# Expert 0's early rows grow from 256 to 384, and the row splits move ahead of the weight conversion, in an attention, mixture-of-experts and MLP kernel

## The chip, the cores and the metric

The kernel runs on one core of a Trainium2 chip. Its five engines each work through their own stream in order: TensorE (PE) multiplies, VectorE (DVE), ScalarE (ACT) and GpSimd (POOL) work on tiles, SyncE (SP) issues DMAs. The metric is the time of one execution on the device in microseconds, the median of several.

## The reference

The inputs are all float32. Sliding-window attention (window 128, ALiBi slopes) over 4 batches, 8 heads and 576 positions of 64 gives 2304 tokens of 512. Each token goes to two of eight experts, and a dense MLP follows:

```python
attn_out = _attn_ref(**attn_kwargs)
x = attn_out.transpose(0, 2, 1, 3).reshape(B * S, H * D)      # 2304 x 512
noisy = x @ w_gate + log1p(exp(x @ w_noise)) * noise          # 2304 x 8
top2, top2_w = the two largest of noisy and their softmax
for e in range(8):                                            # F = 1024
    for k in range(2):
        mask = top2[:, k] == e
        out[mask] += top2_w[mask, k, None] * (relu(x[mask] @ w1[e]) @ w2[e])
h = relu(out @ w_in)                                          # 2048 wide
return h * h @ w_out
```

## The kernel before

**Arithmetic.** A float32 operand is held as two parts, a rounded one (written by ACT) and the remainder (a subtraction on DVE or POOL). A product is three matmuls (`mm3`, L734). So each weight tile needs an ACT cast (L725) and a subtraction on DVE or POOL (L729; POOL does it in four pieces), and each tile of 126 or 128 token rows a cast and a DVE subtraction (`split_x`, L758 and L759, tile `turned`). This last pair is called the row split below.

**Stages.** Attention runs for 18 row tiles. Beside it, a side stream of small steps routes each group of tiles: `logits` and `route` find a token's two experts and its slot in each expert's list, POOL scatters the token numbers to `ids_dram`. The code is written with generators; each `yield` hands the turn back, and `wait` yields five times so that an engine further on has finished. Then come the experts. For each expert 630 slots are computed, in five row tiles.

**Expert 0** starts before all tokens are routed. Its first 256 rows come from the tokens of the first 12 row tiles (`EARLY`, `ET`): `early_rows` loads their list positions, gathers the rows by an indirect DMA on POOL's queue and joins the two 16-bit planes in which rows are stored (`together`, L427); `early_turn` transposes them on PE into the tile `x` or `ps_x` and splits them. `first_expert` then runs all eight slices f of the hidden dimension on these 256 columns (the early stage: `hA` 128x256 and `y` for two row tiles), then the same on the other 374 columns (the late stage: `hA` 128x374 and `y` for three row tiles). The late rows are gathered once all tokens are routed, joined, transposed and split in `late_turn`. Behind the late stage is a branch (`overflow`, L866), which ACT and the others reach in their own order.

**Experts 1 to 7** run one iteration for each slice f. PE does `hA` (374 columns), `hB` (256 columns), then the second product of the slice before (`y`, five row tiles, 15 matmuls). The tile `hB` has one PSUM buffer. Beside this, `fetch` gathers the next expert's rows, transposes them by DMA, and `prepare` joins one row tile (ACT, L427) and splits the one joined an iteration earlier. At f=7 the fifth and last row tile is split. The results `y` are copied out of PSUM after f=7, tiles 0, 2, 4 by ACT and 1, 3 by DVE (L838).

**The conversion.** The dense MLP's weights arrive as 64-bit floats; 32 half tiles are converted to float32 in 32 of the iterations (`HALVES`: six of every eight), by one ACT pass (L1092) and six DVE instructions (`convert_half`, L1104 to L1109). The order on PE, DVE, ACT and SP is the order in which the program is written; POOL's is set by a scheduler.

Of the kernel before, what the change touches and what calls it, by code (L numbers as in the profile page):

```python
# [8 lines left out]
F32 = mybir.dt.float32  # L9
# [12 lines left out]
P = 128  # L22
# [16 lines left out]
EARLY, ET = 12, 2  # L39
# [13 lines left out]
def wait():  # L53

    for _ in range(HOP):
        yield
# [16 lines left out]
class Kernel:  # L73
# [363 lines left out]
    def logits(self, x, lgs):  # L437
# [9 lines left out]
        lg = self.ps_tr.tile([P, 2 * NE], F32, name="ps_lg", tag="ps_tr")  # L447
# [5 lines left out]
    def route(self, vt0, n, lgs):  # L453
# [41 lines left out]
        while self.counted < vt0:  # L495
            yield
# [63 lines left out]
    def attention(self):  # L560
# [58 lines left out]
        def finish(vt, x):  # L619
# [123 lines left out]
    def gather(self, e, j, known=NT):  # L743
        xg = self.rwork.tile([P, DM], F32, name="x", bufs=XB)
        self.nc.gpsimd.indirect_dma_start(
            out=xg.bitcast(U16), out_offset=None, in_=self.x_dram[:known * P, :],
            in_offset=bass.IndirectOffsetOnAxis(ap=self.ids[:, e, j, 0:1], axis=0))
# [77 lines left out]
    def expert_b(self, e, fs, js=range(5)):  # L825

        nc = self.nc
        for j in js:
# [7 lines left out]
            if fs[-1] == 7:  # L836
# [4 lines left out]
                    out_offset=bass.IndirectOffsetOnAxis(ap=self.ids[:n, e, j, 1:2], axis=0),  # L841
# [9 lines left out]
    def count_tiles(self, counts):  # L851
# [5 lines left out]
        nc.vector.tensor_scalar(tiles[:, NE:NE + 1], counts[:, 1, 0:1], float(EARLY_ROWS), float(ET),  # L857
                                op0=ALU.is_lt, op1=ALU.mult)
# [53 lines left out]
    def load_ids(self, e, j0, j1):  # L912

        rows = self.ids_dram[e * REG + j0 * P:e * REG + j1 * P, :]
        self.nc.sync.dma_start(self.ids[:, e, j0:j1], rows.rearrange("(j p) o -> p j o", p=P))

    def early_rows(self):

        while self.scattered < EARLY:
            yield  # L920
        for _ in range(10):
            yield
        self.load_ids(0, 0, ET)
        for _ in range(14):
            yield
        for j in range(ET):
            self.xg[j] = self.gather(0, j, EARLY)
            yield
        for _ in range(8):
            yield  # L930
        for j in range(ET):
            x = self.rwork.tile([P, DM], F32, name="x", bufs=XB)
            self.xg[j] = self.together(self.xg[j], x, self.nc.vector.tensor_copy)
            yield
# [7 lines left out]
    def early_step(self, i):  # L942
# [3 lines left out]
        elif i == 4:  # L946
            self.early_turn(0)
            self.early_turn(1)
            self.split_weights(2, self.nc.vector)

    def settle(self):
# [4 lines left out]
        tot = self.ps_tr.tile([P, 2, NE], F32, name="ps_tot", tag="ps_tr")  # L956
        for i, vt in enumerate((NT, EARLY)):
            nc.tensor.matmul(tot[:, i, :], self.ones16, self.before[:, vt, :], start=True, stop=True)
        yield from wait()
        counts = self.const.tile([P, 2, NE], I32, name="counts")  # L960
# [272 lines left out]
```

## Time and profile before

| | before |
|---|---|
| three runs | 1108.34, 1106.16, 1117.47 us (median 1108.34) |
| the profiled execution | 1101.99 us, its span 1100.2 us |
| PE busy | 1036.5 us, 94% of the span |
| DVE, ACT, POOL busy | 534.4, 485.2, 483.5 us (49, 44, 44%) |
| mean granted clock of PE | 0.957 of full speed |
| attention until | about 206 us |
| expert 0, early stage, then late stage | 208.5 to 234.6 us, 246.5 to 279.9 us |
| experts 1 to 7 | from 283.3 us |

A row of a timeline gives the start, the duration, the engine with the line and the operation, what it writes and reads, and in brackets how long the engine had been idle before and which instruction ended that. A row of the waits adds such idle times up by pair. PE carries nearly all of the span, so a microsecond counts only where PE waits, or where PE runs below its full clock.

### The profile page before, as it was taken

What the parts mean: (1) busy time and instruction counts of PE and PEld (TensorE: products, weight loads), DVE (VectorE), ACT (ScalarE), POOL (GpSimd) and SP (SyncE); (2) the same over time, 40 slices, a digit from 0 to 9 for tenths busy, and PEclk for the clock granted to TensorE, in tenths of its full rate; (3) what the DMA queues carried; (4) which work ended last, traced back from release to release, by engine and by line L of the source; (5) the groups of instructions that cost most, each with busy time, mean ns of one, the idle gap of its engine ahead of it and who ended that gap; (6) DMA issues with size and microseconds to landing.
All of it is one profiled execution on the core that took longest, in us unless ns stands there. A gap on an engine that the chain in (4) does not pass through costs nothing.

```text
span 1100.2 us, 17058 instructions
## 1 busy us (share of the span) xinstructions
PE 1036.5 (94%) x6264; PEld 931.6 (85%) x6264; DVE 534.4 (49%) x1353; ACT 485.2 (44%) x897; POOL 483.5 (44%) x558
## 2 busy tenths in 40 slices
PE   4798989979899999998999999999999999999998
PEld 3687778869788989897888988899999999999997
DVE  7779687642357576756574421562232322223211
ACT  4678586435345454543453532553333333323322
POOL 5356464434466676665566563322222222222221
PEclk7879898789999999998999999999999999999999
DMA  9999993266495958586767422211212221031101
GB/s 200 173 177 207 192 170 102 79 151 158 129 208 172 212 185 215 192 216 188 185 170 199 113 67 72 72 39 34 73 20 67 48 68 39 10 83 33 29 1 29
DMA packets 204269, 131.43 MB, mean 119 GB/s; under 512 B 123108, under 2 KB 180580, under 8 KB 204176
## 3 DMA queue, kind: packets, MB, share of 16 engines
q1 hardware_dynamic: 195312, 109.39, 42.3%
q0 software_dynamic: 8864, 20.86, 6.9%
q8 instruction: 51, 0.84, 0.3%
q14 instruction: 42, 0.34, 0.1%
HBM read 84.56 MB, written 19.95 MB: 95 GB/s over the span
## 4 chain that ended last, share of the span: by engine, by line
PE 58%; DVE 5%; DMA 4%; issue 3%; POOL 2%; ACT 1%; SPq 0%; POOLq 0%; ACTq 0%; DVEq 0%
PE y L734 30%; PE h L734 18%; PE hA L734 6%; PE hB L734 5%; DMA raw<-in_moe_w_out_dram 2%; DVE turned L759 1%; POOL ring L729 1%; DMA y_dram<-xT,ids 1%; DVE raw L1108 1%; DVE store L1105 1%; DVE store L1106 1%; DMA raw<-in_moe_w_in_dram 1%; DVE raw L1107 1%; POOL first L729 0%; DVE hh L820 0%
## 5 line engine op out<-in xcount | busy, mean ns | idle before, releaser
L1141 POOL TENSOR_TENSOR hh<-relu,hh 128x384 fp32r<-128x384 f32 x96 | 97.2, 1013 | 296.9 <-ACT hh L1140 296.9
L1138 DVE SCALAR_TENSOR_TENSOR relu<-h,relu 128x384 f32<-128x384 f32 x96 | 53.5, 557 | 246.6 <-ACT relu L1137 246.6
L734 PE MATMUL y<-first,hh 128*126 128x512 f32 (+2 forms) x642 | 158.8, 396 | 0.0
L734 PE MATMUL y<-ring,hh 128*126 128x512 f32 (+1 forms) x612 | 151.7, 396 | 0.3 <-POOL hh L1141 0.3
L734 PEld LDWEIGHTS y<-first,hh 128*126 128x126 f32 (+2 forms) x642 | 117.7, 188 | 24.4 <-ACT hh L819 0.3
L734 PEld LDWEIGHTS y<-ring,hh 128*126 128x126 f32 (+1 forms) x612 | 112.9, 189 | 23.7 <-POOL hh L1141 0.8
L1137 ACT ACTIVATE relu<-h 128x384 f32<-128x384 f32 x96 | 47.1, 491 | 192.8 <-PE h L734 192.8
L729 POOL TENSOR_TENSOR first<-raw,first 128x256 fp32r<-128x256 f32 x116 | 97.0, 866 | 68.7 <-ACT first L725 55.6
L729 POOL TENSOR_TENSOR ring<-raw,ring 128x256 fp32r<-128x256 f32 x108 | 93.3, 893 | 52.1 <-ACT ring L725 41.7
L734 PE MATMUL y<-store,hh 128*128 128x512 f32 (+1 forms) x444 | 114.7, 397 | 0.0
L734 PE MATMUL h<-turned,store 128*128 128x384 f32 x552 | 107.4, 337 | 0.0
L734 PEld LDWEIGHTS h<-turned,store 128*128 128x128 f32 x552 | 98.1, 188 | 4.0
L734 PEld LDWEIGHTS y<-store,hh 128*128 128x128 f32 (+1 forms) x444 | 83.7, 190 | 15.3
L820 DVE SCALAR_TENSOR_TENSOR hh<-hA,hh 128x374 fp32r<-128x374 f32 (+3 forms) x76 | 39.8, 523 | 99.6 <-ACT hh L819 99.4
L734 PE MATMUL hA<-turned,first 128*128 128x374 f32 (+3 forms) x444 | 82.0, 335 | 4.2 <-ACTq L866 3.5
L734 PEld LDWEIGHTS hA<-turned,first 128*128 128x128 f32 x444 | 76.7, 194 | 7.9 <-ACTq L866 3.9
L1140 ACT CAST hh<-relu 128x384 fp32r<-128x384 f32 x96 | 49.3, 514 | 69.3 <-DVE relu L1138 65.5
L734 PE MATMUL hA<-turned,ring 128*128 128x374 f32 (+3 forms) x420 | 74.6, 327 | 0.0
L734 PEld LDWEIGHTS hA<-turned,ring 128*128 128x128 f32 x420 | 70.5, 188 | 3.0
L353 ACT ACTIVATE prob<-neg,least 128x256 f32<-128x256 f32 (+2 forms) x144 | 61.4, 473 | 9.3 <-DVE least L346 7.7
L759 DVE TENSOR_TENSOR turned<-x,turned 128x504 fp32r<-128x504 f32 (+2 forms) x41 | 41.1, 1004 | 47.3 <-ACT turned L758 47.1
L359 PE MATMUL ps_pt<-identf,prob 128*128 128x128 f32 (+1 forms) x256 | 49.2, 315 | 14.4 <-DVE den L408 11.4
(202 smaller groups left out, 1952.1 us busy)
## 6 DMA issues: line engine op xcount, KB each, us to landing
raw<-in_moe_w_dram SPq DMA_DIRECT2D x128, 256.0 KB, 3.7
raw<-y_dram SPq DMA_DIRECT2D x18, 512.0 KB, 4.0
raw<-in_moe_w_in_dram SPq DMA_DIRECT2D x16, 512.0 KB, 5.7
raw<-in_moe_w_out_dram SPq DMA_DIRECT2D x16, 512.0 KB, 5.8
vraw<-in_v_dram SPq DMA_DIRECT2D x36, 128.0 KB, 5.5
x_dram<-xn SPq DMA_DIRECT2D x18, 256.0 KB, 3.3
out_dram<-osb SPq DMA_DIRECT2D x36, 128.0 KB, 2.4
qraw<-in_q_dram SPq DMA_DIRECT2D x7, 512.0 KB, 4.9
```

The source lines that it names most:

```text
L353: self.nc.scalar.activation(u.p[:, a, :u.w], u.neg[:, a, :u.w], AF.Exp, bias=u.least[:, a:a + 1], scale=-1.0)
L359: self.nc.tensor.transpose(u.pt[:n, a, ci, :], u.p[:, a, ci * P:ci * P + n], self.identf)
L729: engine.tensor_sub(w[1][:, c], raw[:, c], w[0][:, c])
L734: self.nc.tensor.matmul(out, a(x), b(y), start=first and i == 0, stop=last and i == 2)
L759: self.nc.vector.tensor_sub(dst[:, 1, :, col:col + n], x[:, :, :n], dst[:, 0, :, col:col + n])
L820: nc.vector.scalar_tensor_tensor(hh[:, 1], ps, 0.0, hh[:, 0], op0=ALU.max, op1=ALU.subtract)
L1105: nc.vector.tensor_scalar(a, a, 3, 0x3FFFFFFF, op0=ALU.logical_shift_left, op1=ALU.bitwise_and)
L1106: nc.vector.scalar_tensor_tensor(a, hi, -0x40000000, a, op0=ALU.bitwise_and, op1=ALU.bitwise_or)
L1137: nc.scalar.activation(r, ps, AF.Relu)
L1138: nc.vector.scalar_tensor_tensor(r, ps, 0.0, r, op0=ALU.max, op1=ALU.mult)
L1140: nc.scalar.copy(hh[:, 0, :], r)
L1141: nc.gpsimd.tensor_sub(hh[:, 1, :], r, hh[:, 0, :])
```

## The change

Six things change together.

- `EARLY` becomes one number of known row tiles for each early tile (12, 12 and 14), and the early rows 384. Tile 2 is gathered once 14 row tiles are routed, and joined at the start of expert 0, right ahead of its transposes. The late stage keeps 246 columns, two row tiles.
- `route` is stepped by `paced`: three of its small steps a turn instead of one, while `wait` still waits whole turns.
- The logits go into the PSUM tile of the transposes.
- Expert 0's list positions get a tile of their own, `ids0`.
- The fetching of expert 1's rows starts one turn earlier, and its `prepare` follows after two turns instead of three.
- In `experts`, `prepare` (the row split) is written ahead of `convert_half`.

```diff
-EARLY, ET = 12, 2
+EARLY = 12, 12, 14
+ET = len(EARLY)
...
     for _ in range(HOP):
-        yield
+        yield True
+def paced(steps, n=3):
+    i = 0
+    for turn in steps:
+        i = (i + 1) % n
+        if turn or i == 0:
+            yield
...
-        lg = self.ps_tr.tile([P, 2 * NE], F32, name="ps_lg", tag="ps_tr")
+        lg = ps[:, 0, :2 * NE]
...
-                routes.append(self.route(starts[g], GROUPS[g], mine))
+                routes.append(paced(self.route(starts[g], GROUPS[g], mine)))
...
-        self.ids = self.const.tile([P, NE, 5, 2], I32, name="ids")
+        self.ids0 = self.const.tile([P, 5, 2], I32, name="ids0")
+        self.ids = self.const.tile([P, NE - 1, 5, 2], I32, name="ids")
...
     def early_rows(self):
-        while self.scattered < EARLY:
-            yield
-        for _ in range(10):
-            yield
-        self.load_ids(0, 0, ET)
...
+        for known in sorted(set(EARLY)):
+            js = [j for j in range(ET) if EARLY[j] == known]
+            while self.scattered < known:
+                yield
+            for _ in range(10):
+                yield
+            self.load_ids(0, js[0], js[-1] + 1)
+            for _ in range(14):
+                yield
+            for j in js:
+                self.xg[j] = self.gather(0, j, known, self.y_tile())
+                yield
+            if known < EARLY[-1]:
+                for _ in range(16):
+                    yield
+                for j in js:
+                    self.early_join(j)
+                    yield
+    def early_join(self, j):
+        x = self.rwork.tile([P, DM], F32, name="x", bufs=XB)
+        self.xg[j] = self.together(self.xg[j], x, self.nc.vector.tensor_copy)
...
-        elif i == 4:
-            self.early_turn(0)
-            self.early_turn(1)
+        for j in range(ET):
+            if i == (4 if EARLY[j] == EARLY[-1] else 3):
+                if i == 4:
+                    self.early_join(j)
+                self.early_turn(j)
+        if i == 4:
             self.split_weights(2, self.nc.vector)
...
                 for j in rest:
                     self.late_turn(j)
+                self.fetch(1, 0)
...
         self.expert_b(0, (7,), early)
-        self.fetch(1, 0)
         self.expert_a(0, 0, (1,))
         for f in range(8):
+            self.fetch(1, f + 1)
...
-            self.fetch(1, f + 1)
-            self.prepare(1, f + 1, 3)
+            self.prepare(1, f + 1)
...
+            if e + 1 < NE:
+                self.prepare(e + 1, f)
             if n - 1 in HALVES:
                 self.convert_half(HALVES.index(n - 1))
-            if e + 1 < NE:
-                self.prepare(e + 1, f)
```

The first place is DVE where attention ends and expert 0 starts. `turned<-ps_x` is the subtraction of an early row split, `den`, `x` and `xn` finish the last attention tile, `sp_` and `oh` are routing. Before:

```order
696 L422 COPY xn<-x 128x1024
697 L498 TENSOR_TENSOR before<-before,m 128x8
698 L464 TENSOR_SCALAR sp_u<-sp_e 128x8
699 L498 TENSOR_TENSOR before<-before,m 128x8
700 L502 TENSOR_TENSOR gd<-top 128x2
701 L759 TENSOR_TENSOR turned<-ps_x,turned 128x4x128 x2
702 L729 TENSOR_TENSOR first<-raw,first 128x1024
```

And in the changed kernel (the line numbers are those of its own text; L770 is L759 before, L438 is L427, L740 is L729):

```order
697 L770 TENSOR_TENSOR turned<-ps_x,turned 128x4x128 x2
698 L419 TENSOR_TENSOR den<-ps_av,eps 128x4
699 L421 RECIPROCAL den<-den 128x4
700 L423 TENSOR_TENSOR x<-ps_av,den 128x256
701 L433 COPY xn<-x 128x1024
702 L475 TENSOR_SCALAR sp_u<-sp_e 128x8
703 L523 TENSOR_TENSOR oh<-oh,ps_rk 128x32
704 L526 TENSOR_REDUCE sl<-oh 128x4
705 L438 COPY x<-xT 128x2x512
706 L770 TENSOR_TENSOR turned<-ps_x,turned 128x4x128
707 L740 TENSOR_TENSOR first<-raw,first 128x1024
```

The two row splits now stand ahead of the last attention tile, and the third tile's join (`x<-xT`, L438) and split stand behind it and behind three routing steps.

The second place is DVE in an iteration of expert 1 with a conversion and a row split. Before:

```order
897 L820 SCALAR_TENSOR_TENSOR hh<-hA,hh 128x374
898 L820 SCALAR_TENSOR_TENSOR hh<-hB,hh 128x256
899 L1104 TENSOR_SCALAR store<-store 128x512
900 L1105 TENSOR_SCALAR store<-store 128x512
901 L1106 SCALAR_TENSOR_TENSOR store<-raw_5794,store 128x512
902 L1107 TENSOR_SCALAR raw_5794<-store 128x512
903 L1108 SCALAR_TENSOR_TENSOR raw_5794<-raw_5794 128x512
904 L1109 TENSOR_TENSOR store<-store,raw_5794 128x512
905 L759 TENSOR_TENSOR turned<-x,turned 128x4x126
906 L820 SCALAR_TENSOR_TENSOR hh<-hA,hh 128x374
```

And in the changed kernel (L831 is L820 before, L1132 to L1137 are the conversion, L1104 to L1109):

```order
901 L831 SCALAR_TENSOR_TENSOR hh<-hA,hh 128x374
902 L831 SCALAR_TENSOR_TENSOR hh<-hB,hh 128x256
903 L770 TENSOR_TENSOR turned<-x,turned 128x4x126
904 L1132 TENSOR_SCALAR store<-store 128x512
905 L1133 TENSOR_SCALAR store<-store 128x512
906 L1134 SCALAR_TENSOR_TENSOR store<-raw_5781,store 128x512
907 L1135 TENSOR_SCALAR raw_5781<-store 128x512
908 L1136 SCALAR_TENSOR_TENSOR raw_5781<-raw_5781 128x512
909 L1137 TENSOR_TENSOR store<-store,raw_5781 128x512
910 L831 SCALAR_TENSOR_TENSOR hh<-hA,hh 128x374
```

The split stands ahead of the six instructions of the conversion. The same exchange is found at 21 places: at f = 3, 4, 6 and 7 of experts 1 to 5 and once in expert 6. PE's and ACT's orders are the same there.

## Rows read from the trace of the kernel before

**Rows 1.** Waits of PE, 200 to 640 us: total, times, longest.

```profile
PE hB L734 <- DVE turned L759: 8.5, 5, 5.4
PE x L754 <- DVE x L427: 5.3, 1, 5.3
PE hA L734 <- ACTq L866: 3.5, 1, 3.5
```

**Rows 2.** Timeline where expert 0 starts.

```profile
205.94 0.16 DVE L408 TENSOR_TENSOR den<-ps_av,eps 128x4 f32<-128x4 f32 x1 [1.52 <-PE ps_av L400]
...
206.81 0.69 DVE L422 COPY xn<-x 128x1024 uint16<-128x1024 uint16 x1
...
207.81 1.33 DVE L759 TENSOR_TENSOR turned<-ps_x,turned 128x512 fp32r<-128x512 f32 x2
...
208.48 0.58 PE L734 MATMUL hA<-turned,first 128*128 128x256 f32 x1 [0.68 <-ACT turned L758]
```

**Rows 3.** Timeline of the early stage's last slice and the late rows.

```profile
233.07 1.57 PE L734 MATMUL y<-store,hh 128*128 128x512 f32 x6
...
239.15 0.74 DVE L427 COPY x<-x 128x1024 uint16<-128x1024 uint16 x1 [5.04 <-DMA x<-x_dram,ids]
239.94 1.12 PE L754 MATMUL x<-identf,x 128*128 128x128 f32 x4 [5.30 <-DVE x L427]
...
246.47 3.79 PE L734 MATMUL hA<-turned,first 128*128 128x374 f32 x20
```

**Rows 4.** Timeline of the late stage.

```profile
269.32 1.05 ACT L725 CAST ring<-raw 128x1024 fp32r<-128x1024 f32 x1 [0.97 <-PE y L734]
...
273.45 1.05 ACT L725 CAST ring<-raw 128x1024 fp32r<-128x1024 f32 x1 [0.97 <-PE y L734]
...
274.57 3.29 POOL L729 TENSOR_TENSOR ring<-raw,ring 128x256 fp32r<-128x256 f32 x4 [0.84 <-ACT ring L725]
...
276.22 0.49 ACT L819 ACTIVATE hh<-hA 128x374 fp32r<-128x374 f32 x1
...
278.56 1.35 ACT L427 COPY x<-xT 128x1024 uint16<-128x1024 uint16 x1 [1.85 <-DMA xT<-x]
```

**Rows 5.** Timeline where expert 2 starts (f=0 from 341.59, f=1 from 349.39).

```profile
341.59 2.21 PE L734 MATMUL hA<-turned,first 128*128 128x374 f32 x12
...
342.57 0.61 ACT L758 CAST turned<-x 128x504 fp32r<-128x504 f32 x1
...
344.51 1.59 PE L734 MATMUL hB<-turned,first 128*128 128x256 f32 x11 [0.59 <-DVE turned L759]
...
347.13 0.43 DVE L1104 TENSOR_SCALAR store<-store 128x512 f32<-128x512 f32 x1 [0.16 <-ACT store L1092]
...
349.39 2.21 PE L734 MATMUL hA<-turned,ring 128*128 128x374 f32 x12
...
349.97 0.69 DVE L1109 TENSOR_TENSOR store<-store,raw 128x512 f32<-128x512 f32 x1
...
350.54 2.85 POOL L729 TENSOR_TENSOR first<-raw,first 128x256 fp32r<-128x256 f32 x4 [2.87 <-ACT first L725]
350.58 1.28 DVE L838 COPY xT<-y 126x512 f32<-126x512 f32 x2
...
352.86 0.40 PE L734 MATMUL y<-first,hh 128*126 128x512 f32 x1
```

**Rows 6.** Timeline of DVE, a conversion beside four pieces of POOL.

```profile
320.90 0.92 DVE L1104 TENSOR_SCALAR store<-store 128x512 f32<-128x512 f32 x1
...
325.91 0.69 DVE L1109 TENSOR_TENSOR store<-store,raw 128x512 f32<-128x512 f32 x1
```

**Rows 7.** Timeline of the longest wait for a row split.

```profile
513.15 3.18 DVE L1105 TENSOR_SCALAR store<-store 128x512 int32<-128x512 int32 x1
513.26 2.79 POOL L729 TENSOR_TENSOR first<-raw,first 128x256 fp32r<-128x256 f32 x4
...
519.62 2.72 PE L734 MATMUL hB<-turned,first 128*128 128x256 f32 x11 [5.44 <-DVE turned L759]
```

More of the change, by code (lines that the diff above doesn't have):

```diff
@@ L495, in route @@
         while self.counted < vt0:
-            yield
+            yield True
         for v in range(vt0, vt0 + n):
@@ L741, in span, with gather @@
         return j * n, min(n, CAP - j * n)
-    def gather(self, e, j, known=NT):
-        xg = self.rwork.tile([P, DM], F32, name="x", bufs=XB)
+    def gather(self, e, j, known=NT, xg=None):
+        xg = self.rwork.tile([P, DM], F32, name="x", bufs=XB) if xg is None else xg
         self.nc.gpsimd.indirect_dma_start(
             out=xg.bitcast(U16), out_offset=None, in_=self.x_dram[:known * P, :],
-            in_offset=bass.IndirectOffsetOnAxis(ap=self.ids[:, e, j, 0:1], axis=0))
+            in_offset=bass.IndirectOffsetOnAxis(ap=self.ids_of(e)[:, j, 0:1], axis=0))
         return xg
@@ L856, in count_tiles @@
         nc.vector.tensor_scalar(tiles[:, :NE], tiles[:, :NE], 7, None, op0=ALU.logical_shift_right)
-        nc.vector.tensor_scalar(tiles[:, NE:NE + 1], counts[:, 1, 0:1], float(EARLY_ROWS), float(ET),
-                                op0=ALU.is_lt, op1=ALU.mult)
+        for i, known in enumerate(sorted(set(EARLY))):
+            rows = P * sum(k <= known for k in EARLY)
+            late = tiles[:, NE + i:NE + i + 1]
+            nc.vector.tensor_scalar(late, counts[:, 1 + i, 0:1], float(rows), float(ET), op0=ALU.is_lt, op1=ALU.mult)
+        nc.vector.tensor_tensor(tiles[:, NE:NE + 1], tiles[:, NE:NE + 1], late, op=ALU.max)
         nc.vector.tensor_reduce(tiles[:, NE + 1:], tiles[:, :NE + 1], axis=AX.X, op=ALU.max)
@@ L914, in load_ids, with ids_of @@
         rows = self.ids_dram[e * REG + j0 * P:e * REG + j1 * P, :]
-        self.nc.sync.dma_start(self.ids[:, e, j0:j1], rows.rearrange("(j p) o -> p j o", p=P))
+        self.nc.sync.dma_start(self.ids_of(e)[:, j0:j1], rows.rearrange("(j p) o -> p j o", p=P))
+    def ids_of(self, e):
+        return self.ids[:, e - 1] if e else self.ids0
     def early_rows(self):
-        while self.scattered < EARLY:
-            yield
-        for _ in range(10):
-            yield
-        self.load_ids(0, 0, ET)
[L924 to L934, printed above, removed]
+        for known in sorted(set(EARLY)):
[19 more added lines that the diff above has]
+        self.xg[j] = self.together(self.xg[j], x, self.nc.vector.tensor_copy)
     def early_turn(self, j):
@@ L955, in settle @@
             yield
-        tot = self.ps_tr.tile([P, 2, NE], F32, name="ps_tot", tag="ps_tr")
-        for i, vt in enumerate((NT, EARLY)):
+        known = sorted(set(EARLY))
+        tot = self.ps_tr.tile([P, 1 + len(known), NE], F32, name="ps_tot", tag="ps_tr")
+        for i, vt in enumerate((NT, *known)):
             nc.tensor.matmul(tot[:, i, :], self.ones16, self.before[:, vt, :], start=True, stop=True)
         yield from wait()
-        counts = self.const.tile([P, 2, NE], I32, name="counts")
+        counts = self.const.tile([P, 1 + len(known), NE], I32, name="counts")
         nc.vector.tensor_copy(counts, tot)
```

4 lines of the change are left out of this document (2 added, 2 removed).

## The prediction

> **What bounds the kernel.** PE is busy for 94% of the span, so I first asked which waits of PE the changed places can touch: the waits by pair [rows 1]. Three matter: 8.5 us in five waits of `hB` for the row split `turned`, 5.3 us for the join of the late rows, and 3.5 us at the branch behind expert 0. Then the timeline at each place: the start of expert 0 [rows 2], the hole before the late stage [rows 3], the late stage [rows 4], the start of an expert [rows 5], and how long DVE's conversion takes beside POOL [rows 6, 7].
>
> All terms are relative to the profiled execution, 1101.99 us; the median of the three runs is 6.35 us above it, and the sum is moved up by that at the end. A measurement of this kernel can tell about 1% (11 us) from no change.
>
> **The change part by part.**
>
> *Start of expert 0: +5.4.* Before, DVE ends the two splits at 209.14 and PE starts `hA` at 208.48, since the first slice needs only ACT's half at first [rows 2]. Now `hA` covers 384 columns and also needs the third tile, whose join stands on DVE behind the two splits, behind `den` to `xn` (205.94 to 207.50, 1.56 us of work) and behind three routing instructions (0.2 each, sized by `den`'s 0.16) [rows 2]. So: 209.14 + 1.56 + 0.6 = 211.3; the join 0.74, four transposes 1.12 [rows 3], an ACT cast 0.6 [rows 5]: about 213.8 against 208.48. Lower bound: DVE gets `den` to `xn` done in the gap before the splits, as before, since their inputs come at 205.9; then the join ends at 210.5 and `hA` starts at 212.2, +3.7. Upper bound: the gather of the tile is late; its scatters come two tiles after those of the first two, +7. I take +5.4, since the order on DVE is written out.
>
> *Work moved to the early stage: 0.* 128 columns and one row tile per slice go from late to early; PE does the same multiplications.
>
> *The hole before the late stage: −9.4.* PE ends the early stage's `y` at 234.64 and starts the late `hA` at 246.47: 11.83 us [rows 3]. What stays of it is the last early `y` (about 1.4, sized by the 1.57 of the row before it) and eight transposes instead of twelve, behind dense work and so at about half of the 1.12 per four: 1.05. The late rows arrive when routing is through, not when PE is: at 239 to 244, as now. But the early stage starts 5 us later and is 11 us longer (half of an early slice more, 256/374 of 4.13 [rows 4] is 2.8, so 1.4 in each of eight), so PE reaches this point near 250, and the rows wait for PE. So 2.45 of 11.83 remains. Bounds: −10.5 (the `y` hides the transposes) and −6 (the late rows share POOL's queue with expert 1's gathers and come later).
>
> *The late stage: +3.9.* PE now needs 246/374 of 4.13 us per slice (the distance of two casts [rows 4]), that is 2.7 to 2.8. ACT needs, from the cast at 273.45 to the end of `hh` at 276.71, 3.26 us [rows 4], and POOL 3.29 for its four pieces. So with six slices having a weight split, ACT and POOL lose 0.5 per slice, about 3. Behind that, the third DMA transpose of expert 1's rows stands behind a weight load that waits for an earlier split; the copy of such rows waits 1.85 even now [rows 4]. I add 0.9. Bounds 0 (PE is two slices behind its needs, and buffers absorb it) and +8.
>
> *The branch: −1.5.* PE waits 3.5 there for ACT's queue [rows 1]. One row split fewer stands in front of it. Bounds 0 and −3.5.
>
> *The order of row split and conversion: +6.* This is the largest unknown. Before, DVE does the conversion while it would wait anyway for ACT's cast of the row tile; at the start of expert 2 the last split then ends so that `hB` starts at 344.51 [rows 5]. Now DVE waits for the cast, which ends 1.6 us into the *next* slice at an expert's start (343.18 less 341.59), and about 2.8 into it in others, and only then converts. DVE's own price: a split 0.69 (two in 1.33 [rows 2]), a conversion 3.53 alone (347.13 to 350.66 [rows 5]) and 5.70 beside POOL (320.90 to 326.60 [rows 6]); I take 4.3 and, by the same stretching, 1.0 for a split. A slice is 7.0 long (`hA` and `hB` 3.47, from 349.39 to 352.86 [rows 5], and `y` as much).
>
> In a slice in the middle the chain is: cast 2.8, split to 3.8, conversion to 8.1, the two `hh` (about 0.9) to 9.0. `hB` of the slice after needs its buffer at 7.0 + 2.05 = 9.05. It just holds; it misses by some tenths where POOL is in the way. At an expert's start it does not hold: the split of f=7 is behind the conversion of f=6, so it ends 3.2 into the slice and `hB` waits 1.1; then come two conversions in a row before the copies of `y1` (4.3 + 0.9 + 4.3 behind 3.2, then 0.7: 13.4, or 5.3 us into f=1 as it then starts), while PE wants that buffer at 3.47 + 0.7 = 4.2. The second conversion now lies in f=1, where POOL's four pieces start 1.15 us in and last 2.85 [rows 5], so it is nearer to 5.2 than 4.3, and PE waits 1.1 to 2.0. Before, the copies were done at 351.86, 1.7 us before PE's second `y` (352.86 + 0.7) [rows 5]. So per start 1.1 + 1.55 = 2.65, at five starts 13.3, less the 8.5 that it replaces and less 1.1 or more that the `hB` behind the longest wait lost (2.72 against 1.59 [rows 5, 7]): +3.5; and 16 slices in the middle at 0.15: +2.5. Bounds: −9 (no wait remains) and +17 (4 us per start and 0.4 in each other slice).
>
> *The rest: +1.* Routing in larger steps, logits in the same tile, `ids0`: these lie under PE's attention work, which is dense; if the cover fails it costs some us in either direction (−3 to +3). ACT's pass at the head of the conversion waits for its DMA now and then and may do so more often: +1.
>
> Sum: 5.4 − 9.4 + 3.9 − 1.5 + 6 + 1 = +5.4, hence 1107.4 for a profiled execution and about 1114 as a median.
>
> [...] The conversion beside POOL's pieces stretches by 0.36 per instruction (5.70 against 3.53 over six) [rows 5, 6], as if the two engines took turns; once, though, one instruction took 3.18 us and ended as POOL's four pieces did [rows 7]. [...]
>
> **The rivals.**
>
> *A. The split ahead pays (faster).* If conversions run near 3.5, the chain at an expert's start is: split of f=6 to 3.5, conversion to 7.0, `hh` to 7.9 (0.9 in the next slice), split from 1.6 to 2.3, `hB` waits 0.25; two conversions and `hh` later `y1` is copied 3.9 into f=1, before 4.2. The five waits shrink to 1.3 and the term is −8.5 − 1.1 + 1.3 = −8.3. Where POOL is that little in the way the late stage keeps up too (0). Sum 5.4 − 9.4 − 1.5 − 8.3 = −13.8: median 1094.5. It decides where a conversion stays under about 3.8 us. For it: most conversions at the start of expert 2 took 3.5 [rows 5]. Against it: they then lay outside POOL's pieces, and now lie in them. Chance 0.2.
>
> *B. It cancels.* Late stage +1, splits +1, the other terms as above: −3.5, median 1105. For it: every estimate of a wait above is a difference of two long chains. Chance 0.2.
>
> [...] If the second conversion meets POOL's pieces as at 513 us, one instruction takes 3.2 instead of 0.43, `y1` comes 1.3 later than I took, and PE is idle for over 3 us, after which its clock is low: `hB` behind the 5.4 us wait took 2.72 instead of 1.59 [rows 5, 7]. Five starts at 1.3 + 1.1 and more: +14, median 1128. Against it: one such case in some thirty conversions was enough to be seen. Chance 0.13.
>
> *D. The forecast* has 0.47; its own range is 1107 to 1122, by the bounds of start, late stage and split taken half way.
>
> **The numbers.** 1114; range 1097 to 1129, which leaves out most of A and the tail of C. Faster by over 1% (below 1097.3): most of A, 0.19. Slower by over 1% (above 1119.4): C and a good third of D, 0.13 + 0.17 = 0.30. Within 1%: 0.51.
>
> **What would show it.** In the profile after: `hA` of expert 0 starting near 213 to 214, waiting for the third tile's chain; no wait for the late rows' join; in the late stage waits of `hA` or `y` on ACT or POOL; at the starts of experts 2 to 6 a wait of `y` for the copies by DVE, and a wait of `hB` for `turned` near 1 us. It is wrong if conversions stay at 3.5 (then A), if `hB` of slices in the middle waits for `hh` by more than some tenths (slower), or if the gathers of the third tile come after 211.

## The result and the profile after

| | before | changed |
|---|---|---|
| median of 20 runs | 1108.69 us (1096.11 to 1118.13) | 1116.82 us (1108.38 to 1122.12) |
| ratio, 95% interval | | 1.010 (1.0071 to 1.0128) |
| span of the profiled execution | 1100.2 us | 1109.3 us |
| PE busy | 1036.5 us | 1037.9 us |

The changed kernel is 1% slower, with the same work on PE. Where the 9.1 us of the two profiled spans went, from the starts of PE's instructions in the two timelines (the forecast's terms beside them; the 11 us that move from the late stage to the early one are the forecast's estimate):

| stretch | before | after | difference | forecast |
|---|---|---|---|---|
| start to the first transposes of early rows | 205.83 | 206.94 | +1.1 | +1 (the rest) |
| these to expert 0's first `hA` | 2.65 | 7.77 | +5.1 | +5.4 |
| to the late stage's first `hA` | 37.99 | 39.66 | +1.7: 11 moved in, −9.3 for the hole | −9.4 |
| late stage, to its last `y` | 33.38 | 32.29 | −1.1: 11 moved out, +9.9 lost | +3.9 |
| to expert 1's first `hA` | 3.49 | 3.74 | +0.25 | −1.5 |
| expert 1 | 58.25 | 54.30 | −3.95 | |
| experts 2 to 6 | 289.76 | 295.56 | +5.8 | +6 |
| expert 7 and the MLP | 468.85 | 469.04 | +0.2 | |

The 3.95 us of expert 1 are one slice (f=5) that took 11.3 us in this execution of the kernel before; it is long in some profiles of either order and not in others, so it says nothing about the change. Nor is the +1.1 of the first row more than one pair of profiles: in five other runs with the changed code up to that point the transposes start at 211.8 to 214.7 us, in two others with the old code at 206.8 and 210.3.

The waits of PE after the change, 195 to 660 us (total, times, longest), answer to [rows 1]:

```profile
PE y L745 <- DVE xT L849: 10.7, 5, 2.2
PE y L745 <- ACT hh L830: 5.6, 3, 2.9
PE hA L745 <- ACTq L880: 3.7, 1, 3.7
PE ps_x L765 <- DVE x L438: 3.1, 1, 3.1
...
PE hB L745 <- DVE turned L770: 0.5, 3, 0.2
```

The 8.5 us of `hB` and the 5.3 us of the late join are gone, and in their place stand 10.7 us of `y` behind DVE's copies, 5.6 us behind ACT in the late stage, and 3.1 us behind the third tile's join. The start of expert 0, answering to [rows 2]:

```profile
206.94 1.97 PE L765 MATMUL ps_x<-identf,x 128*128 128x128 f32 x8
...
208.71 0.69 DVE L770 TENSOR_TENSOR turned<-ps_x,turned 128x512 fp32r<-128x512 f32 x1 [3.03 <-ACT turned L769]
...
210.17 0.15 DVE L419 TENSOR_TENSOR den<-ps_av,eps 128x4 f32<-128x4 f32 x1
...
212.07 0.73 DVE L438 COPY x<-xT 128x1024 uint16<-128x1024 uint16 x1
...
212.95 1.08 PE L765 MATMUL ps_x<-identf,x 128*128 128x128 f32 x4 [3.08 <-DVE x L438]
...
214.71 0.69 PE L745 MATMUL hA<-turned,first 128*128 128x384 f32 x1 [0.68 <-ACT turned L769]
```

The join at 212.07 has no idle time before it: it stood behind `den` to `xn` and the three routing steps. DVE had idled for 3.03 us just before 208.71. The hole before the late stage, answering to [rows 3]:

```profile
249.91 1.36 ACT L438 COPY x<-x 128x1024 uint16<-128x1024 uint16 x1
...
251.41 1.04 PE L765 MATMUL x<-identf,x 128*128 128x128 f32 x8
```

The late rows are joined without a wait, and PE has none before their transposes. The late stage, answering to [rows 4] (SPq is the DMA queue of SyncE):

```profile
264.86 1.24 SPq L796 DMA_TRANSPOSE xT<-x  x1
...
270.33 1.33 ACT L438 COPY x<-xT 128x1024 uint16<-128x1024 uint16 x1 [4.09 <-DMA xT<-x]
...
272.04 0.36 ACT L830 ACTIVATE hh<-hA 128x246 fp32r<-128x246 f32 x1
...
272.46 2.24 PE L745 MATMUL y<-ring,hh 128*128 128x512 f32 x6 [2.90 <-ACT hh L830]
```

ACT's copy of an expert 1 row tile waits 4.09 us for its DMA transpose, `hh` stands behind it on ACT, and PE's `y` behind `hh`; the six matmuls after the wait take 2.24 us, where those at 266.62 take 1.55, and the granted clock after it is low, 0.67 of full speed on average against 1.00 before (columns of this view: the stretch, then busy time and count of PE, PEld, DVE, ACT and POOL, then the clock, DMA's share and GB/s):

```profile
268.00:272.40 4.40, 1.56 (x13) 1.35 (x11) 0.23 (x1) 2.06 (x4) 1.17 (x2) 1.00 0.90 234
272.40:277.50 5.10, 5.00 (x20) 4.21 (x21) 2.08 (x4) 5.10 (x8) 4.08 (x6) 0.67 0.50 135
```

Where the late stage ends, ACT's last instruction ahead of the branch is the copy of the last `y`, which itself waited for PE; PE's next `hA` starts at 290.40:

```profile
286.70 0.59 ACT L849 COPY xT<-y 118x512 f32<-118x512 f32 x1 [2.43 <-PE y L745]
```

Last, DVE and PE at the start of expert 3 (f=0 from 404.60, f=1 from 411.97), answering to [rows 5]:

```profile
406.22 0.82 DVE L770 TENSOR_TENSOR turned<-x,turned 128x504 fp32r<-128x504 f32 x1
...
406.96 0.96 DVE L1132 TENSOR_SCALAR store<-store 128x512 f32<-128x512 f32 x1
...
411.19 0.69 DVE L1137 TENSOR_TENSOR store<-store,raw 128x512 f32<-128x512 f32 x1
...
412.58 0.42 DVE L1132 TENSOR_SCALAR store<-store 128x512 f32<-128x512 f32 x1
...
413.11 4.12 POOL L740 TENSOR_TENSOR ring<-raw,ring 128x256 fp32r<-128x256 f32 x4 [2.31 <-ACT ring L736]
...
416.68 1.10 DVE L1137 TENSOR_TENSOR store<-store,raw 128x512 f32<-128x512 f32 x1
...
417.71 1.27 DVE L849 COPY xT<-y 126x512 f32<-126x512 f32 x2
...
418.44 3.03 PE L745 MATMUL y<-ring,hh 128*126 128x512 f32 x12 [2.14 <-DVE xT L849]
```

Two conversions in a row (4.9 and 5.2 us), the second of them beside POOL's pieces, and only then the copies: PE waits 2.14 us for the first of them.

### The profile page after: what moved, and what is told of

It reads as the page before. It is cut to its first block, busy times and chain, and to the rows that moved or that the text cites. A ratio compares the mean times of both kernels' runs of the same rounds, so it can differ in the third digit from the quotient of the medians.

```text
span 1109.3 us, 17092 instructions
## 1 busy us (share of the span) xinstructions
PE 1037.9 (94%) x6265; PEld 928.0 (84%) x6265; DVE 530.4 (48%) x1355; ACT 485.2 (44%) x897; POOL 479.5 (43%) x558
## 4 chain that ended last, share of the span: by engine, by line
PE 61%; DVE 7%; issue 3%; ACT 1%; DMA 1%; POOL 1%; DVEq 0%; ACTq 0%; POOLq 0%
PE y L745 31%; PE h L745 17%; PE hA L745 7%; PE hB L745 5%; DVE store L1134 1%; DVE raw L1136 1%; DVE store L1132 1%; DMA y_dram<-xT,ids 1%; DVE turned L770 1%; DVE raw L1135 1%; DVE hh L831 1%; DVE store L1133 1%; ACT x L438 0%; DVE store L1137 0%; DVE xT L849 0%
## 5 line engine op out<-in xcount | busy, mean ns | idle before, releaser
L745 PE MATMUL y<-first,hh 128*126 128x512 f32 (+2 forms) x642 | 161.7, 400 | 7.1 <-DVE xT L849 6.4
L745 PE MATMUL y<-ring,hh 128*126 128x512 f32 (+2 forms) x612 | 151.9, 395 | 7.7 <-DVE xT L849 4.2
L745 PEld LDWEIGHTS y<-ring,hh 128*126 128x126 f32 (+2 forms) x612 | 111.8, 187 | 32.2 <-DVE xT L849 5.1
L740 POOL TENSOR_TENSOR first<-raw,first 128x256 fp32r<-128x256 f32 x116 | 93.6, 837 | 73.6 <-ACT first L736 67.2
L740 POOL TENSOR_TENSOR ring<-raw,ring 128x256 fp32r<-128x256 f32 x108 | 87.7, 845 | 68.8 <-ACT ring L736 66.2
L831 DVE SCALAR_TENSOR_TENSOR hh<-hA,hh 128x374 fp32r<-128x374 f32 (+2 forms) x76 | 39.8, 523 | 104.7 <-ACT hh L830 101.2
L745 PE MATMUL hA<-turned,first 128*128 128x374 f32 (+2 forms) x444 | 83.4, 338 | 4.4 <-ACTq L880 3.7
L745 PEld LDWEIGHTS hA<-turned,first 128*128 128x128 f32 x444 | 77.3, 195 | 8.4 <-ACTq L880 4.5
L770 DVE TENSOR_TENSOR turned<-x,turned 128x504 fp32r<-128x504 f32 (+2 forms) x40 | 36.1, 907 | 100.7 <-ACT turned L769 100.7
L745 PE MATMUL hA<-turned,ring 128*128 128x374 f32 (+2 forms) x420 | 74.6, 327 | 0.0
L736 ACT CAST first<-raw 128x1024 fp32r<-128x1024 f32 x32 | 33.4, 1048 | 65.1 <-PE y L745 53.4
```

The lines of the kernel that those rows point to most:

```text
L736: self.nc.scalar.copy(w[0], raw)
L740: engine.tensor_sub(w[1][:, c], raw[:, c], w[0][:, c])
L745: self.nc.tensor.matmul(out, a(x), b(y), start=first and i == 0, stop=last and i == 2)
L770: self.nc.vector.tensor_sub(dst[:, 1, :, col:col + n], x[:, :, :n], dst[:, 0, :, col:col + n])
L831: nc.vector.scalar_tensor_tensor(hh[:, 1], ps, 0.0, hh[:, 0], op0=ALU.max, op1=ALU.subtract)
```

## The experiments

Each was timed beside the kernel before on the same chip; the ratio is to that. A profiled execution varies where the experiment changes nothing: with the changed code up to that point, the first transposes start between 206.9 and 214.7 us. So the traces are compared by stretches, not by spans. The table counts, for the 40 slices of experts 2 to 6, the time over 6.95 us a slice, and how long SyncE's queue stood before a load of 64-bit weights until a conversion had freed its buffer.

| kernel | ratio (95%) | f=0 | f=1 | f=2 to 7 | SyncE's wait |
|---|---|---|---|---|---|
| before | 1 | 11.5 | 0.1 | 0.1 | 2.5 |
| changed | 1.0100 (1.0071 to 1.0128) | 2.3 | 14.7 | 0.6 | 19.6 |
| swap_undone | 1.0013 (0.9975 to 1.0050) | 6.8 | 0.0 | −0.1 | 1.3 |
| before_swap | 1.0099 (1.0065 to 1.0133) | 2.2 | 15.1 | 0.2 | 19.1 |
| copies_first | 1.0029 (0.9991 to 1.0067) | 2.3 | −0.1 | 11.3 | 19.1 |
| act_copies | 1.0163 (1.0112 to 1.0214) | 2.1 | −0.1 | 10.3 | 19.4 |
| halves | 1.0192 (1.0147 to 1.0237) | 2.2 | 0.0 | 21.9 | 32.5 |
| before_halves_swap | 1.0199 (1.0156 to 1.0243) | 2.1 | 0.1 | 20.9 | 30.6 |
| lag3 | 1.0053 (1.0023 to 1.0082) | 2.8 | 12.3 | 1.8 | 20.0 |
| join_first | 1.0137 (1.0091 to 1.0183) | 2.2 | 15.0 | 0.1 | 19.2 |
| two_tiles | 1.0101 (1.0062 to 1.0139) | 2.2 | 15.1 | 0.4 | 19.1 |
| unpaced | 1.0097 (1.0060 to 1.0133) | 2.2 | 16.1 | 1.0 | 19.4 |
| undone_lag3_join | 1.0060 (1.0027 to 1.0093) | 13.4 | 0.0 | 0.0 | 1.4 |
| halves_lag3_unpaced_join | 1.0119 (1.0075 to 1.0163) | 2.2 | −0.1 | 20.1 | 30.5 |

### The exchange undone, and the exchange alone

```diff
 swap_undone: the changed kernel
+            if n - 1 in HALVES:
+                self.convert_half(HALVES.index(n - 1))
             if e + 1 < NE:
                 self.prepare(e + 1, f)
-            if n - 1 in HALVES:
-                self.convert_half(HALVES.index(n - 1))
 before_swap: the kernel before, with these lines exchanged the other way
```

> The changed kernel with the row split put back behind the conversion. Theory 1 (the backlog): the 10.7 us in which PE waits at five expert starts for DVE's copies of y come from two conversions in a row that the exchange puts ahead of them; they vanish here, and the five waits of hB for the row split come back (0.5 to 1.3 us each, one of them larger if a conversion is blocked). The starts of experts 2 to 6 cost 6 to 16 us over plain slices instead of 17, and the time is 1 to 10 us below the changed kernel. Theory 2 (the start and the late stage of expert 0 carry the whole loss, the exchange is neutral): within 2 us of the changed kernel.

> The kernel before with the exchange alone: the row split ahead of the conversion in experts 1 to 6. Theory 1 (the backlog): at each start of experts 2 to 6 hB waits about 0.4 us instead of 0.6 to 1.3 and y waits about 2 us for DVE's copies, 17 us over plain slices in all against 11.5 before; 3 to 6 us slower than before, ratio 1.003 to 1.006. Theory 2 (the exchange is neutral or a gain): the same as before or 3 us faster, with waits of y for the copies absent, since they need the third early tile.

Without the exchange the changed kernel is within 0.5% of the kernel before; the exchange alone makes the kernel before slower by as much as the whole change. The waits of PE in `before_swap` (283 to 640 us) show that the third tile has no part in the waits of `y`:

```profile
PE y L734 <- DVE xT L838: 10.7, 5, 2.2
PE hB L734 <- DVE hh L820: 5.5, 1, 5.5
PE hA L734 <- ACTq L866: 3.5, 1, 3.5
PE hB L734 <- DVE turned L759: 0.3, 2, 0.2
```

The first row is that of the changed kernel to the tenth. In `swap_undone` it is gone, and the waits for the split are back:

```profile
PE hB L745 <- DVE turned L770: 5.5, 5, 1.7
```

So theory 1 of the two runs stands, and theory 2 falls: the exchange is the main loss, and by `swap_undone` all other parts together come to 0.1% (−0.3 to +0.5%). The traces lean to the upper end of that: from the first transposes to expert 1 five kernels with the changed code there take 82.5 to 84.9 us, and three with the old code 77.5 to 79.6. The exchange's size was above what was expected of `before_swap` (1.003 to 1.006).

### The copies taken out of the queue, in two ways

```diff
 copies_first: the changed kernel
-            if n - 1 in HALVES:
+            if n - 1 in HALVES and f:
                 self.convert_half(HALVES.index(n - 1))
             if 8 < n < 8 * NE - 1:
                 e, f = divmod(n - 1, 8)
                 self.expert_b(...)
+            if n - 1 in HALVES and n % 8 == 0:
+                self.convert_half(HALVES.index(n - 1))
 act_copies: the changed kernel
-                (nc.vector.tensor_copy if j % 2 else nc.scalar.copy)(ysb[:n], y)
+                nc.scalar.copy(ysb[:n], y)
```

> The changed kernel with one thing moved: in the first slice of an expert (f=0) the conversion stands behind DVE's two copies of y instead of ahead of them. Theory 1 (the backlog of two conversions ahead of the copies): the waits of y for the copies vanish at all five starts, the waits of hB for the split stay near 0.4 us, the second slice falls from 9.3 to 10.8 us to 7.0, and the time falls by 12 to 15 us, to about 1103. Rival (contention with POOL: the conversion in the second slice is stretched wherever it stands, and whatever is behind it is late): the copies come in time, but the hh of the second slice comes late and hB or y waits for it by 1 to 2 us; a fall of 5 us at most.

> The changed kernel with all five y tiles copied out of PSUM by ACT instead of three by ACT and two by DVE; the split stays ahead of the conversion, and the conversion stays where it is. Theory (the copies are late because they queue on DVE behind two conversions): the waits of y for DVE's copies vanish, the slice behind an expert's first falls from 9.3 to 10.9 us to 7.0 to 8.0 (ACT's own five copies take 2.6 us there and may cost some tenths), and unlike the kernel with the conversion put behind the copies nothing frees the 64-bit buffers later, so no new wait of hB for hh comes up. 10 to 15 us below the changed kernel. Rival (DVE is short of time in these slices whatever it does first): the slices behind stay at 8.5 us or more with waits of hB or y for DVE's hh; 5 us or less.

In both the waits of `y` are gone and f=1 is a plain slice, as the theory said. But 10 to 11 us come back in other slices. PE's first wait between 283 and 640 us, of `copies_first` and then of `act_copies`:

```profile
PE hB L745 <- DVE hh L831: 10.5, 6, 3.1
```

```profile
PE hB L745 <- DVE hh L831: 8.9, 5, 3.1
```

In time `copies_first` has gained on the changed kernel (1.0029, and the two intervals do not overlap), but some 8 us where its theory had 12 to 15; `act_copies` has not (1.0163), and its trace, in which experts 2 to 6 take 290.4 us against 295.6 in the changed kernel, does not show why. The rival, which `act_copies` was to exclude, named the right kind of wait, of `hB` for `hh`, though in another place: the slices of 8.3 to 10.3 us are at f=5. Its reason (DVE has no time) is not what the timeline of `act_copies` shows for expert 2's f=4 and 5 (from 381.23 and 388.18) and for SyncE's queue ahead of them:

```profile
360.33 0.38 SPq L1109 DMA_DIRECT2D raw<-in_moe_w_in_dram  x1
...
365.12 1.12 DVE L1137 TENSOR_TENSOR store<-store,raw 128x512 f32<-128x512 f32 x1
...
369.39 1.24 SPq L796 DMA_TRANSPOSE xT<-x  x1
...
377.31 0.38 SPq L1112 DMA_DIRECT2D raw<-in_moe_w_out_dram  x1
...
382.67 0.67 ACT L1120 ACTIVATE store<-raw 128x512 f32<-128x512 f32 x1 [4.32 <-DMA raw<-in_moe_w_out_dram]
...
385.40 0.60 ACT L769 CAST turned<-x 128x504 fp32r<-128x504 f32 x1
...
386.04 1.00 DVE L770 TENSOR_TENSOR turned<-x,turned 128x504 fp32r<-128x504 f32 x1 [7.24 <-ACT turned L769]
386.96 0.97 DVE L1132 TENSOR_SCALAR store<-store 128x512 f32<-128x512 f32 x1
...
392.71 1.70 PE L745 MATMUL hB<-turned,first 128*128 128x256 f32 x12 [2.34 <-DVE hh L831]
```

DVE stands idle for 7.24 us. It waits for ACT's cast, and ACT was held 4.32 us by the load of 64-bit weights that was issued at 377.31. That load did not wait for its buffer: there are two, and the conversion that used this one before ended at 366.24. SyncE came to it late. It issued nothing from 360.71 to 369.39, where it sends a transpose of the next expert's rows, and the load stands behind that in its queue. What SyncE waited for at this one the view does not name; three other such transposes in this trace wait for the scatter of `y` (283 to 640 us):

```profile
SPq L796 <- DMA y_dram<-xT,ids: 25.6, 3, 8.7
```

In the changed kernel the same load goes out at 368.62, 5.7 us into f=2, and here 3.0 us into f=3; there PE's wait had made f=1 10.84 us long instead of 6.93, and the queue had that time.

Late loads cost PE nothing at f=1 to 7 in the old order (in the table 0.1 and 0.1 us for `before`, 0.0 and −0.1 for `swap_undone`). Yet ACT waits for its 64-bit loads 27.0 us in all in the kernel before and 25.9 in `swap_undone`, against 24.9 in `act_copies` and 17.3 in the changed kernel (283 to 640 us). At the same place `swap_undone` has:

```profile
381.50 0.66 ACT L1120 ACTIVATE store<-raw 128x512 f32<-128x512 f32 x1 [2.77 <-DMA raw<-in_moe_w_out_dram]
...
382.19 0.43 DVE L1132 TENSOR_SCALAR store<-store 128x512 f32<-128x512 f32 x1 [3.00 <-ACT store L1120]
...
386.92 1.22 DVE L770 TENSOR_TENSOR turned<-x,turned 128x504 fp32r<-128x504 f32 x1
```

The conversion starts as soon as ACT's pass is through, while ACT goes on to the cast. With the split ahead, the conversion waits for the cast as well, which ended 2.66 us after the pass in `act_copies`, and `hh` stands behind both.

The exchange also makes a conversion hold its buffer longer. From the issue of its load to the end of its conversion it is 10.9 us in the median of the 32 in the kernel before (and in `swap_undone`), and 15.6 to 15.7 in the changed kernel, `before_swap` and `act_copies`. The difference is the exchange itself: from the end of ACT's pass to the end of the conversion it takes 8.7 us in the median, where it took 4.1, since the conversion now stands behind the split. At an expert's start SyncE then waits for the buffer. One case of the changed kernel (a load, the last instruction of its conversion, and the next load into the same buffer):

```profile
396.20 0.38 SPq L1109 DMA_DIRECT2D raw<-in_moe_w_in_dram  x1
...
411.19 0.69 DVE L1137 TENSOR_TENSOR store<-store,raw 128x512 f32<-128x512 f32 x1
...
411.91 0.38 SPq L1109 DMA_DIRECT2D raw<-in_moe_w_in_dram  x1
```

The buffer is free at 411.88, and the next load is issued at 411.91. In `swap_undone` a load at 400.96 was converted by 411.91. That these waits of SyncE cost PE time is not shown: they come to 19 to 20 us in the changed kernel and in `copies_first` alike, and the loads for which ACT waits longest in `copies_first` and `act_copies` (five in each, 3.3 to 4.7 us) had had a free buffer for 9 to 11 us.

### Other places for the conversions

```diff
 halves: the changed kernel; before_halves_swap: the same on before_swap
-HALVES = [n for n in range(8, 8 * NE) if n % 8 in (0, 2, 3, 5, 6, 7)][:32]
+HALVES = [n for n in range(8, 8 * NE) if n % 8 in (1, 2, 3, 4, 5, 6)][:32]
```

> The changed kernel with other slices for the conversions: those of f = 2 to 7 of an expert carry one and those of f = 0 and 1 none, so that at most one conversion stands ahead of the copies of y and two slices are free for catching up. The split stays ahead of the conversion. Theory (the exchange costs time because the conversions of f = 6, 7 and 0 pile up in front of the copies and free the two 64-bit buffers late): the waits of y for the copies vanish, the waits of hB for the split stay at 0.4 us, no wait of hB for hh takes their place, and the time falls by 9 to 15 us to the level of the kernel before or 3 us below it. Rival (DVE has no room for the exchange wherever the conversions lie, as the kernels with earlier copies suggest): the waits move into the six slices in a row, where hB waits for hh by 1 us or more each expert; a fall of 0 to 5 us.

> The kernel before with two things different: the split ahead of the conversion, and the conversions in the slices f = 2 to 7. Theory (the exchange is a gain where conversions do not pile up at an expert's start): 5 to 9 us below the kernel with the exchange alone, and 2 to 7 us below the kernel before (its waits of hB for the split, 8.5 us, fall to about 0.4 us at each start); ratio to before 0.994 to 0.999. Rival: ratio 1.003 or more, with waits of hB for hh.

The theory as written fell in both: no wait for copies, and yet 21 to 22 us lost in f=2 to 7 and a ratio of 1.019 to 1.020. ACT's waits in `halves` (283 to 640 us) name the place, and SyncE's queue waits longer for conversions than in any other kernel here:

```profile
ACT store L1120 <- DMA raw<-in_moe_w_in_dram: 62.6, 15, 7.9
```

```profile
SPq L1112 <- DVE store L1137: 17.5, 10, 3.2
SPq L1109 <- DVE store L1137: 15.0, 5, 3.7
```

In the kernel before that queue waits 2.5 us for conversions in all. But of ACT's ten longest waits the five of 5.6 to 7.9 us are for loads whose buffer had been free for 17 us, and the other five (3.0 to 4.6) for loads whose buffer had been free for 1.6 to 1.7. So the buffers may have a part in the second five and have none in the first. Why so much is lost with these places stays open: the places with the old order of split and conversion were not run, and neither was a third buffer.

### Expert 0's late stage

```diff
 lag3: the changed kernel
-            self.prepare(1, f + 1)
+            self.prepare(1, f + 1, 3)
```

> The changed kernel with one thing put back: in expert 0's late stage the rows of expert 1 are joined three turns after their gather and not two. Theory (ACT stands still): PE's waits of 2.9 and 2.3 us for ACT's hh come from ACT's copy of such a row tile, which waits 4.1 and 2.1 us for its DMA transpose, and the low clock after them costs as much again; with a turn more the copies wait under 1 us, and the time falls by 6 to 9 us, less 1 us for the split that is left ahead of the branch. Rival (throughput: ACT and POOL need 3.3 us for a slice in which PE needs 2.8): the waits spread over the slices but stay 3 us or more in sum, and the time falls by 0 to 3 us.

The late stage went from 32.3 to 26.1 us in the trace, and the ratio from 1.0100 to 1.0053 (their intervals just overlap). Over the seven kernels with this late stage and two turns it takes 30.8 to 32.3 us, over the three with three turns 26.1 to 26.2. The copy that waited 4.09 us for its transpose is issued a turn later:

```profile
273.39 1.24 SPq L796 DMA_TRANSPOSE xT<-x  x1
...
278.67 1.37 ACT L438 COPY x<-xT 128x1024 uint16<-128x1024 uint16 x1
```

It has no wait. So ACT's standing still made 6.2 of the 9.9 us lost in this stage; the 3.7 left would fit the throughput of ACT and POOL, which no run took apart. The wait at the branch rose from 3.7 to 4.4, which would fit the split left there.

### Expert 0's start, the third tile and the routing's steps

```diff
 join_first: the changed kernel
-        for j in range(ET):
-            if i == (4 if EARLY[j] == EARLY[-1] else 3):
-                if i == 4:
-                    self.early_join(j)
-                self.early_turn(j)
+        if i == 3:
+            self.early_join(ET - 1)
+            for j in range(ET):
+                self.early_turn(j)
 two_tiles: the changed kernel
-EARLY = 12, 12, 14
+EARLY = 12, 12
 unpaced: the changed kernel
-def paced(steps, n=3):
+def paced(steps, n=1):
```

> The changed kernel with the third early tile's join, transposes and split put with those of the first two, ahead of the last attention tile's end on DVE. Theory (the order on DVE makes expert 0 late): its rows have landed by then, since DVE idles 3.0 us there; the first hA starts 3.5 to 4 us after the first transposes instead of 7.8, and 3 to 4.5 us are saved in the trace. Rival (the gather lands late): DVE stands at the join, and with it the last attention tile; the start does not come sooner, and the late rows come later. In time 3 to 4 us at most, close to what can be told.

> The changed kernel with the third early tile taken away: 256 early rows as before, all else as changed. Theory (the third tile gains little, since it costs 5 us at the start and 4 or more in the late stage of the 9 that it saves in the hole): expert 0 starts 5 us sooner, the hole before the late stage is back at about 11 us, the late stage at some 33 us without its waits for ACT; the time is within 4 us of the changed kernel. Rival (the third tile pays for itself): 6 us or more slower than the changed kernel.

> The changed kernel with routing in single steps a turn as before, all else as changed. Theory (the larger steps put DVE's routing work ahead of attention's, so that attention ends some 4 us later than before and the ranks' matmul waits for DVE): the first transposes of the early rows start at 205 to 210 us instead of 207 to 216, and the time falls by 2 to 6 us. Rival (attention's end varies by that much from run to run whatever the routing): the same time within 2 us; or, where the third tile's rows then come later, 2 to 4 us more.

`join_first`: from the first transposes to `hA` it takes 4.3 us instead of 7.8, so the rows had landed and the order on DVE was the cause. But from there to the late stage it takes 45.4 us instead of 39.7, by a new wait in the early stage:

```profile
230.88 0.17 DVE L504 TENSOR_TENSOR m<-oh 128x8 bf16<-128x8 f32 x1
...
231.11 0.19 PE L517 MATMUL ps_rk<-m,tri 128*128 128x8 bf16 x1 [4.87 <-DVE m L504]
```

The matmul of the routing's ranks stands on PE ahead of the expert's, and DVE comes to its input late. It cost more than the start gave. `two_tiles`: the ratio is that of the changed kernel, 1.0101; from the first transposes to expert 1 the trace has 77.3 us instead of 83.5 (and 77.5 in the kernel before). By the traces the third early tile closes a hole of 9 us and opens 15 elsewhere; by the times, which tell 0.4% at best, it neither gains nor loses. `unpaced`: the same ratio again, and the transposes start at 216.4, later than in the changed kernel's profile; the steps of the routing make no difference that these times tell.

### Two versions put together

```diff
 undone_lag3_join: swap_undone, lag3 and join_first together
 halves_lag3_unpaced_join: halves, lag3, unpaced and join_first together
```

> The changed kernel with three things different: the row split back behind the conversion, expert 1's rows joined three turns after their gather, and the third early tile's join and split put ahead of the last attention tile on DVE. Theory (the loss is the exchange, the start's order on DVE and ACT's waits in the late stage, and the 384 rows are a gain without them): expert 0 starts 3 to 4 us sooner after attention, its late stage is 4 to 6 us shorter, the y waits for copies are gone; 6 to 10 us below the kernel before, ratio 0.991 to 0.995. Rival (384 rows gain nothing, since what the hole gives is lost elsewhere): the same as before within 3 us.

> The 384 early rows and the split ahead of the conversion with four things different: the conversions in the slices f = 2 to 7, expert 1's rows joined three turns after their gather, routing in single steps, and the third tile's join ahead of the last attention tile. Theory: the sum of the parts, 0 to 3 below the kernel before for the conversions' places, 4 to 5 for the late stage, 3 to 4 for the start, and the wait of the routing's ranks for DVE (3.9 to 4.9 us in the two kernels with the early join) gone: ratio to before 0.988 to 0.996. Rival (single steps make routing late, so the late rows come after PE wants them): a wait for the late rows' join of 3 us or more, and the same as before.

Both missed. In the first the ranks' matmul waited again (3.9 us, 45.3 us for the early stage), and three of its five expert starts lost 3.5 to 4.3 us to a split that came late behind the conversion, more than in `swap_undone`. In the second the stretch from the first transposes to expert 1 is the shortest of all, 75.3 us (4.6, 40.0, 26.2 and 4.5; with single steps the ranks' matmul does not wait), and the 20 us of the conversions' places outweigh it. That stretch together with the old order of split and conversion, and the old places, was not run. None of these kernels is shown to beat the kernel before.

## Why the prediction was right, and where it was not

The forecast was 1114 us against a median of 1108.34 for the kernel before; measured were 1116.82 against 1108.69. The side holds, and so does the largest term, the order of split and conversion; the size of the whole, 5.7 us, was half of the 11 us of the ratio (8 to 14). Two other terms have the wrong size or sign, and part of the agreement in the table is luck.

- **Start, +5.4: right** (+5.1), and for the reason given; `join_first` shows it.
- **The hole, −9.4: right** (−9.3, with the estimate of 11 us for the work moved). The late rows were joined at 249.9 without a wait, and the eight transposes behind PE's dense work took 1.04 us, where I had 1.05.
- **Late stage, +3.9: mis-sized.** It lost 9.9. The throughput that I put first would be 3.7 of it (I had 3); the wait for the DMA transposes, for which I added 0.9, is 6.2, the low granted clock after each wait included (0.67 of full speed from 272.4 to 277.5, 0.57 from 283.8 to 286.7). I had read that the copy waits 1.85 us even before [rows 4], but not that ACT, with turns of 2.8 us instead of 4.1, would come to the second copy ahead of its transpose. That transpose stood on SyncE's queue behind a weight load (263.84) at which the queue had waited 16.6 us, and it went out at 264.86; the copy starts at 270.33.
- **Branch, −1.5: wrong** (+0.25). One split fewer stands there, but no split ended the wait: ACT's copy of `y` at 286.70 came last, behind PE, and 3.1 of the 3.74 us lie after that copy's end. What fills them no run shows.
- **Exchange, +6: right in kind, too low.** It was to come out at five expert starts as a wait of `hB` near 1 us and one of `y` of 1.1 to 2.0; measured were 0.1 and 2.1. The slices f=0 and 1 lost 3.4 us a start where I had 2.65, the slices in the middle 0.6 us in all where I had 2.5. The step that failed is what I took off: 9.6 us of waits that it replaces, most of them the one start behind the conversion of [rows 7], in which one instruction took 3.18 us, and whose f=0 took 14.34 us. In `swap_undone` the one conversion with such an instruction (3.27 us) lies at f=5, whose slice took 6.93 us all the same, and its five starts lose 6.8 us. So the +5.8 beside my +6 in the table is luck: it rests on that one start in the profile of the kernel before. By the times the exchange costs 11 us (7 to 15) on the kernel before.
- **The rest, +1: not decided.** The profiles have +1.1, but where attention ends varies by more than that between profiles.
- **What I had not seen** is that ACT comes late at f=4 of an expert once PE's wait at f=1 is gone. My chain of a slice in the middle, with the last `hh` at 9.0 us where 9.05 is needed, holds in the changed kernel (0.6 us lost) and breaks there. It did not enter the forecast, since PE shows it only when the copies are out of the way.
- **The rivals.** A needed conversions under 3.8 us; they took 4.9 and 5.2 at a start. B needed the late stage at +1 and the exchange at +1; the late stage came out at +9.9, and the exchange at +5.8 in the profiles and 11 by the times. The sums of A and B leave out the +1 of the rest, so each should stand 1 us higher. C needed an instruction of 3.2 us at each start, as in [rows 7]; no conversion instruction of the changed kernel took over 1.3 us (the longest 1.22). What the rows show is each instruction beside POOL's pieces stretched by 0.4 us (the last three of the conversion at 412.58 took 0.85, 1.11 and 1.10 us, those of the one before it, behind the end of the pieces, 0.43, 0.69 and 0.69), and POOL's four pieces by 1.3 (4.12 against 2.85 [rows 5]). In [rows 7] the DVE instruction starts 0.11 us ahead of POOL's first piece and yet ends after all four, and no run shows what decides between the two. The 1.1 us that C adds a start for PE's clock is that of `hB` in [rows 7], where the granted clock was 0.50 of full speed (519.6 to 522.4), against 1.00 in that of [rows 5] (344.5 to 346.1).

## What to carry to other kernels

When an instruction that waits for another engine is put ahead of a long piece of work on an in-order engine, count how much later that work ends, and then follow what stands behind it: here the copies of `y`, the `hh` of the slice, and the end of a buffer's hold. The wait that shows on the critical engine may hide another: taking it away here brought 10 to 11 of 14.7 us back in other slices. And an engine that another is seen waiting for need not be the late one; before a buffer is blamed, compare when it came free with when its next load was issued. Where turns get shorter, the time between a DMA and the copy of its data shrinks with them, so price the copy's wait by everything in front of that DMA on its queue.

## What the runs showed of the hardware

- The first transposes of the early rows start at 205.8, 206.8 and 210.3 us in the three profiles with the old code up to there (the kernel before, `before_halves_swap`, `before_swap`), and at 206.9 to 214.7 in six with the changed code. A difference of 4 to 8 us in one profile can lie there; whether the changed code makes attention later besides, these profiles do not decide.
- The second instruction of a conversion (0.43 us in the median of 32) once took 3.27 us in `swap_undone` (at 504.41), as it once took 3.18 in the kernel before, beside four pieces of POOL [rows 7]; in the changed kernel it took 0.85 at most.
